# Pooled attention and a routed FFN on one core: the routing and the FFN moved a half pair, small operations swapped between GpSimd and VectorE, the last half reordered

## The chip, the core and the metric

The kernel runs on one core of one Trainium2 chip. The core has five engines that work side by side, each through its own list of instructions in order: TensorE (PE in the profile; its weight loads are a row of their own, PEld), VectorE (DVE), ScalarE (ACT), GpSimd (POOL) and SyncE (SP), which here only issues transfers. The metric is the time of one execution on the device, in microseconds (us); less is better.

## The reference, cut to what matters

All numbers are fp32. There are 8 batches with 8 heads, 1152 keys, and head width 64.

```python
# attention; queries are averaged in pairs: 1152 -> 576 per head
q_pool = q.reshape(B, H, S // 2, 2, D).mean(axis=3)
scores = scale * np.matmul(q_pool, k.transpose(0, 1, 3, 2))
attn = np.exp(scores - max) ; attn = attn / (sum + 1e-9)
attn_out = np.matmul(attn, v)                    # (8, 8, 576, 64)
x = attn_out -> (B, 576, 512)                    # heads side by side

# routed FFN: only 128 of a batch's 576 tokens pass through it
scores = np.einsum('bsd,d->bs', x, w_gate)
out = x.copy()
for b in range(B):
    top_idx = np.argpartition(-scores[b], 128)[:128]
    xe = x[b, top_idx]
    ye = np.maximum(xe @ w1, 0.0) @ w2           # 512 -> 1024 -> 512
    g = 1.0 / (1.0 + np.exp(-scores[b, top_idx]))
    out[b, top_idx] = x[b, top_idx] + g[:, None] * ye
```

## The kernel before

Heads are taken two at a time: 8 batches of 4 pairs make 32 pairs. A pair is worked in two halves of 288 queries, `s` = 0 and 1, so there are 64 halves, and half `h` belongs to pair `h // 2`. In half `h` TensorE computes the scores of half `h` (line 818, 9 blocks of 128 keys, ScalarE takes the exponents, line 825) and then the weighted values of half `h - 1` (line 836). So 8 halves after a batch's first one the next batch begins, and the routing and the FFN of a batch run between the halves of the batches behind it. `p` has two buffers, PSUM is used as four pairs of banks in turn (`banks()`).

What the other engines do in a half, in the order of the program:

```python
    def gated(self, half):              # of half h - 3
        nc.vector.tensor_reduce(pair["red"][:, ns], pair["prod"][:, ns, :], AX.X, ALU.add)   # L979
        if half["s"] == 1:
            nc.vector.tensor_tensor(out=pair["part"][:, pair["hp"], :],                      # L981
                in0=pair["red"][:, :], in1=pair["rec"][:, :], op=ALU.mult)
            if pair["hp"] == self.NPAIR - 1:      # a batch's last pair: its routing begins
                unit = self.routed(pair["b"], pair["part"])
                at = next(unit) == "mid"
                self.routing.append([pair["b"], unit, at])

    def folded(self, half):             # of half h: sums over the keys
        for u in range(G):              # G = 3
            nc.gpsimd.tensor_tensor(out=acc[:, u, :], in0=units[:, 0, u, :],                 # L857
                                    in1=units[:, 1, u, :], op=ALU.add)
        for a, of in enumerate((units[:, 2, :, :], acc[:, :, :])):
            nc.vector.tensor_reduce(fold[:, a, :], ..., apply_transpose=True)                # L862
        nc.vector.tensor_reduce(pair["sum"][:, :, ns], ...)                                  # L872

    # multiplied(h - 2): GpSimd, prod = avb * w_gate (L925)
    # prepare_pair, even halves: GpSimd qp (L732), VectorE transposes kT, qT (L735, L739)
    # weighted(h - 1): TensorE L836; ScalarE copies PSUM to `two` (L844); GpSimd av (L846)
    # drained(h - 1): VectorE transposes av to avb (L915)
    # added, even halves: VectorE `total` of the pair's sums (L893); spread: ScalarE L902

    def normalized(self, pair):         # odd halves
        ...
        rec = pair["rec"] = self.small.tile([P, self.QB], F32, name="rec")
        nc.vector.reciprocal(rec[:, :], tot)                                                 # L954
        x = self.work.tile([P, self.QB, BLK], F32, name="x")
        nc.gpsimd.tensor_tensor(out=x[:, :, :], in0=pair["avb"][:, :, :],                    # L956
            in1=rec[:, :].unsqueeze(2).broadcast_to([P, self.QB, BLK]), op=ALU.mult)
        pair["x"] = x
```

`routed` is a generator: each `yield` ends a piece, and its mark says where in a half the next piece is put. `"mid"` is behind the scores, `True` at the half's end; a false mark goes on at once.

```python
    def routed(self, b, part):
        mid = "mid" if b < self.B - 2 else True
        nc.vector.tensor_reduce(line[:, :], part..., AX.X, ALU.add)                          # L1007
        if b < self.B - 1:
            yield mid
            if b < self.B - 2:
                groups = self.side_by_side(line)          # ScalarE
                yield True
                total = self.added(groups)
            else:                                         # batch 6 alone
                nc.tensor.matmul(ps, lhsT=merge, rhs=line[:, :], ...)                        # L1021
                nc.scalar.copy(total[:, :], ps[0:BLK, :])
            ...                          # scores through DRAM and back as a line on all lanes
            yield True
            if b < self.B - 2:
                yield True
        else:                            # the last batch: diag (VectorE), L1054, columns (L679)
            ...
        for t, rows in tiles:            # ranks by comparison, 5 tiles: L1083, L1092, L1102
            ...
            if t == 1:
                yield True
            if t == 3:
                yield mid
                nc.scalar.activation(gate[:, :], gate[:, :], AF.Exp, scale=-1.0)
                if b < self.B - 2:
                    yield True
        ...                              # rank through DRAM to `lines`
                yield True
                for of, to in ((self.token_line, found), (lines[:, :, 1, :], own_gate)):
                    nc.vector.scalar_tensor_tensor(out=pick..., accum_out=to[0:w, :])        # L1166
                nc.gpsimd.tensor_scalar(out=index[0:w, :], in0=found[0:w, :],                # L1175
                    scalar1=float(b * Sp), scalar2=None, op0=ALU.add)
            nc.gpsimd.indirect_dma_start(out=xe[0:w, :], ...)         # gather of the rows, L1183
            yield True
            yield mid
            ...                          # 4 transposes of xe (L1197), ScalarE copies to xeT
            yield mid
            ...                          # layer 1: 8 pieces (L1208); marks False, last "hidden"
            ...                          # layer 2: 8 pieces (L1221); marks False
            ...                          # times the gate, plus xe, scatter
```

The loop over the halves, before:

```python
        for h in range(n_halves + 1):
            if h < n_halves:
                ...
                self.scores(half)
                ...                                 # side_by_side (even) or spread (odd)
                self.units(mid=True)
                if h > 2:
                    self.gated(halves[h - 3])
                self.folded(half)
                if h > 1:
                    self.multiplied(halves[h - 2])
                if s == 0 and loaded:
                    upcoming = loaded
                    self.prepare_pair(upcoming)
            else:
                self.stored(halves[h - 3]["pair"])
                self.gated(halves[h - 3])
                self.multiplied(halves[h - 2])
                self.units(mid=True)
                self.units(mid=False)
            if h > 0:
                done = halves[h - 1]
                self.weighted(done)
                self.drained(done)
            if h == n_halves:
                self.multiplied(done)
                self.gated(halves[h - 2])
            if 1 < h < n_halves and s == 0:
                done["pair"]["total"] = self.added(done["pair"]["groups"])
            if h == n_halves:
                self.normalized(done["pair"])
            elif h > 2 and s == 1:
                self.normalized(halves[h - 2]["pair"])
            if h < n_halves:
                self.units(mid=False)
```

So, counted from a batch's first half (r = 0), the routing begins at r = 10, the ranks are computed at the ends of r = 13, 14 and 15, the gather is issued at the end of r = 16, and transposes, layer 1 and layer 2 stand in the middle of r = 18, 19 and 20. Batch 5's layer 2 and the FFNs of batches 6 and 7 are kept for the end, where they fill TensorE's time while the last batch is routed.

Of the kernel before, what the change touches and what calls it, by code (L numbers as in the profile page):

```python
# [10 lines left out]
P = 128  # L11
BLK = 32
# [522 lines left out]
class _Plain:  # L535
# [396 lines left out]
    def normalized(self, pair):  # L932

        nc, hp = self.nc, pair["hp"]
        tot = self.sums[:, pair["b"] * self.NPAIR + hp, :]
        if self.last_pair(pair):
            ps = self.banks()[:, 0, :]
            nc.tensor.matmul(
                ps[:, 0 : 2 * self.QB],
                lhsT=self.merge.rearrange("p g j -> p (g j)"),  # L940
                rhs=pair["sum"].rearrange("p j n -> p (j n)"),
                start=True,
                stop=True,
            )
            for j in range(2):
                rows = slice(j * self.D, (j + 1) * self.D)
                nc.scalar.activation(
                    tot[rows, :],
                    ps[rows, j * self.QB : (j + 1) * self.QB],
                    AF.Identity,  # L950
                    bias=self.tiny[rows, 0:1],
                )
        rec = pair["rec"] = self.small.tile([P, self.QB], F32, name="rec")
        nc.vector.reciprocal(rec[:, :], tot)  # L954
        x = self.work.tile([P, self.QB, BLK], F32, name="x")
        nc.gpsimd.tensor_tensor(  # L956
            out=x[:, :, :],
            in0=pair["avb"][:, :, :],
            in1=rec[:, :].unsqueeze(2).broadcast_to([P, self.QB, BLK]),
            op=ALU.mult,  # L960
        )
        pair["x"] = x

    def stored(self, pair):

# [7 lines left out]
    def gated(self, half):  # L973

        nc, pair, hb = self.nc, half["pair"], self.HB
        if half["s"] == 0:
            pair["red"] = self.small.tile([P, self.QB], F32, name="red")
        ns = slice(half["s"] * hb, (half["s"] + 1) * hb)
        nc.vector.tensor_reduce(pair["red"][:, ns], pair["prod"][:, ns, :], AX.X, ALU.add)  # L979
        if half["s"] == 1:  # L980
            nc.vector.tensor_tensor(  # L981
                out=pair["part"][:, pair["hp"], :],
                in0=pair["red"][:, :],
                in1=pair["rec"][:, :],
                op=ALU.mult,
            )
# [10 lines left out]
    def routed(self, b, part):  # L997
# [139 lines left out]
        for s0, w in self.slots:  # L1137
# [3 lines left out]
            if b == self.B - 1:  # L1141

                nc.vector.tensor_tensor(
                    out=pick[:, :, 0:w],
                    in0=self.slot_f[:, s0 : s0 + w].unsqueeze(1).broadcast_to([P, NT, w]),
                    in1=rank[:, :].unsqueeze(2).broadcast_to([P, NT, w]),
                    op=ALU.is_equal,
                )
                yield True
                ps = self.banks()[:, 0, 0:2]  # L1150
                for t, rows in tiles:
                    nc.tensor.matmul(
                        ps[0:w, :],
                        lhsT=pick[0:rows, t, 0:w],
                        rhs=meta[0:rows, t, :],
                        start=(t == 0),
                        stop=(t == NT - 1),
                    )
                nc.scalar.copy(index[0:w, :], ps[0:w, 0:1])
                nc.scalar.copy(own_gate[0:w, :], ps[0:w, 1:2])  # L1160
            else:
                yield True

                found = self.small.tile([P, 1], F32, name="found_token")
                for of, to in ((self.token_line, found), (lines[:, :, 1, :], own_gate)):
                    nc.vector.scalar_tensor_tensor(  # L1166
                        out=pick.rearrange("p t i -> p (t i)").rearrange("p (i t) -> p i t", t=NT)[0:w],
                        in0=lines[0:w, :, 0, :],
                        scalar=self.token[0:w, s0 // P : s0 // P + 1],
                        in1=of[0:w, :, :],  # L1170
                        op0=ALU.is_equal,
                        op1=ALU.mult,
                        accum_out=to[0:w, :],
                    )
# [115 lines left out]
        )  # L1290
        return count_i

    def units(self, mid):


        for entry in self.routing[::-1]:
            b, unit, at = entry
            if b in self.waiting or at != mid:
# [6 lines left out]
            entry[2] = end in ("mid", "hidden") and b < self.B - 2  # L1305

    def run(self):
        nc = self.nc
# [10 lines left out]
            self.load_values(loaded)  # L1319
        self.load_gate()  # L1320
        weights = self.weight_loads()
        for h in range(n_halves + 1):
            if h < n_halves:
                n, s = divmod(h, 2)
                if s == 0:
                    pair = upcoming
                    if pair["hp"] == 0:
                        part = self.ffn.tile([P, self.NPAIR, self.QB], F32, name="part")
                    pair["part"] = part
                else:  # L1330
                    loaded = None
                    if n + 2 < len(pairs):
                        loaded = self.load_pair(*pairs[n + 2])
                        self.load_values(loaded)
                    if n > 1:
                        self.stored(halves[h - 4]["pair"])
                if h > 1:
                    next(weights, None)
                half = {"pair": pair, "s": s}
                halves.append(half)  # L1340
                self.scores(half)
                if h > 1:

                    of = halves[h - 2 - s]["pair"]
                    if s == 0:
                        of["groups"] = self.side_by_side(of["sum"].rearrange("p j n -> p (j n)"))
                    else:
                        self.spread(of)
                self.units(mid=True)
                if h > 2:  # L1350
                    self.gated(halves[h - 3])
                self.folded(half)
                if h > 1:
                    self.multiplied(halves[h - 2])
                if s == 0 and loaded:
                    upcoming = loaded
                    self.prepare_pair(upcoming)
            else:
                self.stored(halves[h - 3]["pair"])
                self.gated(halves[h - 3])  # L1360
                self.multiplied(halves[h - 2])
                self.units(mid=True)
                self.units(mid=False)
            if h > 0:
                done = halves[h - 1]
                self.weighted(done)
                self.drained(done)
            if h == n_halves:
                self.multiplied(done)
                self.gated(halves[h - 2])  # L1370
            if 1 < h < n_halves and s == 0:
                done["pair"]["total"] = self.added(done["pair"]["groups"])
            if h == n_halves:
                self.normalized(done["pair"])
            elif h > 2 and s == 1:
                self.normalized(halves[h - 2]["pair"])
            if h < n_halves:
                self.units(mid=False)
        for _ in weights:
            pass  # L1380

        self.stored(halves[-1]["pair"])


        self.gated(halves[-1])
        left = [unit for _, unit, _ in self.routing]
        new = left.pop()
        old = left.pop() if left else iter(())
        older = left.pop() if left else iter(())
        assert not left  # L1390
# [81 lines left out]
```

## Time and profile before

| | |
|---|---|
| time, median of 3 runs | 707.77 us (707.0 to 708.58) |
| span of the profiled run | 704.8 us |
| first score block starts | 8.8 us |
| last matmul ends | 698.4 us |
| TensorE clock granted | 0.998 |
| HBM traffic | 115 GB/s over the span |

A row of the profile's groups names the line, the engine, the operation, what it writes and reads with their shapes, how often it ran, its busy time in all and the mean of one in ns, and the idle time of the engine just before it with what ended it. These are the groups of the operations that the change touches:

```
L857 POOL TENSOR_TENSOR acc<-p 128x576 f32<-128x576 f32 x192 | 266.3, 1417 | 15.4 <-ACT p L825 15.1
L862 DVE TRANSPOSE_TENSOR_REDUCE fold<-p 128x54 f32<-128x1728 f32 x64 | 126.0, 1969 | 50.2 <-ACT p L825 50.2
L956 POOL TENSOR_TENSOR x<-avb,rec 128x576 f32<-128x576 f32 x32 | 37.1, 1159 | 40.3 <-DVE rec L954 27.9
L981 DVE TENSOR_TENSOR part<-red,rec 128x18 f32<-128x18 f32 x32 | 27.0, 845 | 1.1
L893 DVE TENSOR_REDUCE total<-groups 32x36 f32<-32x144 f32 (+1 forms) x37 | 12.0, 325 | 0.0
L954 DVE RECIPROCAL rec<-sums 128x18 f32<-128x18 f32 x32 | 7.2, 225 | 0.0
L1175 POOL TENSOR_SCALAR index<-found_token 128x1 int32<-128x1 f32 x7 | 6.4, 920 | 20.2 <-DVE pick L1166 20.2
```

The chain that ended last is followed back from the last instruction, at each step to what released it. Printed in order of time it gives start, length and what ran; `x72` are 72 matmuls. The timeline gives start, length, engine, line, operation and operands.

### The profile page before, as it was taken

The numbers are of one execution on the slowest core, as the hardware profiler recorded it, in microseconds if no ns is written. First come the engines' busy times: TensorE is split into PE (matmuls) and PEld (weight loads), VectorE is DVE, ScalarE is ACT, GpSimd is POOL, SyncE is SP. The second block draws the span as 40 slices with busy tenths as digits, with TensorE's granted clock in tenths as the row PEclk, the third lists the DMA queues.
The fourth block names the chain that finished last, engine by engine and source line by source line (L and its number), as shares of the span: only waits on it lengthen the run. The fifth ranks groups of instructions, "written<-read, shape, count | busy, mean of one in ns | idle before, by whom it ended". The sixth has DMA issues, their size and how long they took to land.

```text
span 704.8 us, 23397 instructions
## 1 busy us (share of the span) xinstructions
PE 694.4 (99%) x9948; PEld 516.8 (73%) x9948; DVE 496.5 (70%) x793; ACT 444.5 (63%) x963; POOL 485.1 (69%) x452
## 2 busy tenths in 40 slices
PE   8999999999999999999999999999999999999996
PEld 5668899996758866688656887578775787766573
DVE  3877777996559965498754988559774697689540
ACT  6677778777547775477746776467754777477210
POOL 5877777868658695586955779467874877686520
PEclk9999999999999999999999999999999999999999
DMA  8888887858486483756928468382775728432200
GB/s 175 172 178 180 171 166 137 146 116 161 85 149 111 85 162 75 145 97 111 172 40 159 81 129 160 66 148 61 161 130 85 135 56 169 83 72 62 45 31 35
DMA packets 389490, 82.86 MB, mean 118 GB/s; under 512 B 376640, under 2 KB 376640, under 8 KB 389376
## 3 DMA queue, kind: packets, MB, share of 16 engines
q1 hardware_dynamic: 387872, 76.49, 58.1%
q0 software_dynamic: 1280, 4.20, 1.8%
q8 instruction: 80, 1.31, 0.8%
q10 hardware_dynamic: 224, 0.59, 0.3%
q14 instruction: 34, 0.28, 0.1%
HBM read 69.65 MB, written 11.59 MB: 115 GB/s over the span
## 4 chain that ended last, share of the span: by engine, by line
PE 89%; POOL 5%; issue 2%; DMA 1%; ACT 1%; DVE 1%; SPq 0%; POOLq 0%; DVEq 0%; ACTq 0%
PE ps L836 36%; PE ps L818 36%; PE ps L1208 8%; PE ps L1221 7%; POOL acc L857 2%; ACT p L825 1%; DMA kb<-in_k_dram 1%; DMA xe<-out_dram,index 1%; PE ps L1197 1%; POOL prod L925 1%; POOL x L956 0%; POOL av L846 0%; DVE fold L862 0%; POOL index L1175 0%; SPq L759 0%
## 5 line engine op out<-in xcount | busy, mean ns | idle before, releaser
L825 ACT ACTIVATE p<-ps 128x576 f32<-128x576 f32 x576 | 320.2, 695 | 1.7 <-PE ps L818 1.3
L818 PE MATMUL ps<-qT,kT 64*64 64x288 f32 x4608 | 295.2, 404 | 0.2 <-ACT p L825 0.2
L836 PE MATMUL ps<-p,v_sb 64*64 64x288 f32 x4608 | 294.6, 403 | 0.0
L857 POOL TENSOR_TENSOR acc<-p 128x576 f32<-128x576 f32 x192 | 266.3, 1417 | 15.4 <-ACT p L825 15.1
L836 PEld LDWEIGHTS ps<-p,v_sb 64*64 64x64 f32 x4608 | 215.5, 133 | 65.3 <-ACT p L825 9.2
L818 PEld LDWEIGHTS ps<-qT,kT 64*64 64x64 f32 x4608 | 208.0, 132 | 73.0 <-ACT p L825 15.4
L862 DVE TRANSPOSE_TENSOR_REDUCE fold<-p 128x54 f32<-128x1728 f32 x64 | 126.0, 1969 | 50.2 <-ACT p L825 50.2
L862 DVE TRANSPOSE_TENSOR_REDUCE fold<-acc 128x54 f32<-128x1728 f32 x64 | 125.3, 1957 | 46.0 <-POOL acc L857 45.8
L844 ACT COPY two<-ps 128x576 f32<-128x576 f32 x64 | 40.9, 639 | 156.9 <-PE ps L836 143.8
L846 POOL TENSOR_TENSOR av<-two 128x288 f32<-128x288 f32 x64 | 51.2, 800 | 96.5 <-ACT two L844 94.9
L915 DVE STREAM_TRANSPOSE avb<-av 128x288 f32<-128x288 f32 x64 | 29.4, 460 | 66.5 <-POOL av L846 66.5
L956 POOL TENSOR_TENSOR x<-avb,rec 128x576 f32<-128x576 f32 x32 | 37.1, 1159 | 40.3 <-DVE rec L954 27.9
L1208 PEld LDWEIGHTS ps<-xeT,w 128*128 128x128 f32 x512 | 57.8, 192 | 2.7 <-ACT p L825 2.6
L1208 PE MATMUL ps<-xeT,w 128*128 128x128 f32 x512 | 59.3, 277 | 0.0
L1221 PE MATMUL ps<-w,hT 128*128 128x512 f32 x128 | 57.3, 598 | 0.0
L925 POOL TENSOR_TENSOR prod<-avb,w_gate 128x288 f32<-128x288 f32 x64 | 51.5, 805 | 0.6 <-DVE avb L915 0.6
L902 ACT ACTIVATE sums<-total,tiny 32x18 f32<-32x18 f32 x124 | 38.1, 308 | 15.9 <-DVE total L893 14.2
L732 POOL TENSOR_TENSOR qp<-qb 128x576 f32<-128x576 f32 x31 | 43.8, 1414 | 2.2 <-DMA qb<-in_q_dram 2.2
L1221 PEld LDWEIGHTS ps<-w,hT 128*128 128x128 f32 x128 | 23.6, 190 | 28.1 <-issue 25.8
L735 DVE STREAM_TRANSPOSE kT<-kb 128x1152 f32<-128x1152 f32 x31 | 42.5, 1370 | 0.0
L887 ACT COPY groups<-sum 32x36 f32<-32x36 f32 x124 | 27.1, 219 | 6.7 <-DVE sum L872 5.2
L981 DVE TENSOR_TENSOR part<-red,rec 128x18 f32<-128x18 f32 x32 | 27.0, 845 | 1.1
(95 smaller groups left out, 290.6 us busy)
## 6 DMA issues: line engine op xcount, KB each, us to landing
kb<-in_k_dram SPq DMA_DIRECT2D x124, 144.0 KB
qb<-in_q_dram SPq DMA_DIRECT2D x124, 144.0 KB
v_sb<-in_v_dram SPq DMA_DIRECT2D x124, 144.0 KB
out_dram<-x SPq DMA_DIRECT2D x128, 72.0 KB
lines<-row_rank SPq DMA_DIRECT2D x7, 640.0 KB
w<-in_moe_w_dram SPq DMA_DIRECT2D x8, 512.0 KB
sc_row<-row SPq DMA_DIRECT2D x7, 288.0 KB
acc<-in_q_dram ACTq DMA_DIRECT2D x2, 288.0 KB
```

What stands on the lines that cost most here:

```text
L732: nc.gpsimd.tensor_tensor(out=qp[:, :, :], in0=pair["q"][:, :, 0, :], in1=pair["q"][:, :, 1, :], op=ALU.add)
L735: nc.vector.transpose(kT.rearrange("p (c g i) -> p c g i", c=self.NC, i=BLK), pair["k"].rearrange("p (g c) d -> p c g d", c=self.NC),)
L818: nc.tensor.matmul(sc[keys, j, 0:n], lhsT=pair["kT"][rows, c * P + keys.start : c * P + keys.stop], rhs=pair["qT"][rows, qs], start=True, ...
L825: nc.scalar.activation(p[:, c // G, c % G, :, :], sc[:, :, 0:n], AF.Exp, scale=self.scale)
L836: nc.tensor.matmul(av[j * self.D : (j + 1) * self.D, e, 0:n], lhsT=half["pair"]["v"][keys, j, c, :], rhs=half["p"][keys, c // G, c % G, j, :],
L844: nc.scalar.copy(two[:, :, :], av[:, :, 0:n])
L846: nc.gpsimd.tensor_tensor(out=half["av"][:, :], in0=two[:, 0, :], in1=two[:, 1, :], op=ALU.add)
L857: nc.gpsimd.tensor_tensor(out=acc[:, u, :], in0=units[:, 0, u, :], in1=units[:, 1, u, :], op=ALU.add)
L862: nc.vector.tensor_reduce(fold[:, a, :], of.rearrange("p u (m d) -> p (u m) d", d=BLK), AX.X, ALU.add, apply_transpose=True,)
L925: self.nc.gpsimd.tensor_tensor(out=pair["prod"][:, ns, :], in0=pair["avb"][:, ns, :], in1=self.w_gate[:, hp : hp + 1, :].broadcast_to([P, ...
L1208: nc.tensor.matmul(pv[:, f, 0:w], lhsT=self.w1[:, c, (f0 + f) * P : (f0 + f + 1) * P], rhs=xeT[:, c, 0:w], start=(c == 0), stop=(c == self ...
L1221: nc.tensor.matmul(ps[0:w, 0 : self.Dm], lhsT=hT[:, f, 0:w], rhs=self.w2[:, f, :], start=(f == 0), stop=(f == self.NFC - 1),)
```

## The change

It regroups work without changing what is computed. `x` is computed by GpSimd half a pair later, at the end of the even half. The product of gate sums and reciprocals (`part`) moves from VectorE to GpSimd, except for the last two pairs, so that VectorE is relieved. The token index of the gather is computed by VectorE, so that GpSimd's queue doesn't stand waiting for it, and the gather is issued in the next half behind GpSimd's sums (a new place, `"sums"`, behind `folded`). Transposes and both layers of the FFN of batches 0 to 5 come one half later, to give the gather time. The first piece of the routing, `line`, also goes to the place `"sums"`. `total` is computed ahead of the transposes of the next pair's keys. The last half gets an order of its own, in which the value blocks of the last two halves follow each other and the products for the last batch's routing are ahead of `x`.

The diff, cut (`...`) where lines are only moved or indented:

```diff
-        rec = pair["rec"] = self.small.tile([P, self.QB], F32, name="rec")
-        nc.vector.reciprocal(rec[:, :], tot)
-        x = self.work.tile([P, self.QB, BLK], F32, name="x")
-        nc.gpsimd.tensor_tensor(
+        pair["rec"] = self.small.tile([P, self.QB], F32, name="rec")
+        nc.vector.reciprocal(pair["rec"][:, :], tot)
+
+    def divided(self, pair):
+        x = pair["x"] = self.work.tile([P, self.QB, BLK], F32, name="x")
+        self.nc.gpsimd.tensor_tensor(
...
         if half["s"] == 1:
-            nc.vector.tensor_tensor(
+            ending = pair["b"] == self.B - 1 and pair["hp"] >= self.NPAIR - 2
+            engine = nc.vector if ending else nc.gpsimd
+            engine.tensor_tensor(
                 out=pair["part"][:, pair["hp"], :],
...
             if pair["hp"] == self.NPAIR - 1:
-                unit = self.routed(pair["b"], pair["part"])
-                at = next(unit) == "mid"
-                self.routing.append([pair["b"], unit, at])
+                self.routing.append([pair["b"], self.routed(pair["b"], pair["part"]), "sums"])
...
-                nc.gpsimd.tensor_scalar(
+                nc.vector.tensor_scalar(
                     out=index[0:w, :],
...
+                yield "sums"
             xe = ffn.tile([P, self.Dm], F32, name="xe")
             nc.gpsimd.indirect_dma_start(
...
             yield True
-            yield mid
+            if b < self.B - 2:
+                yield True
+            if b != self.B - 2:
+                yield mid
...
-        for h in range(n_halves + 1):
+        for h in range(n_halves):
...
+            self.units("mid")
+            if h > 2:
                 self.gated(halves[h - 3])
+            self.folded(half)
+            self.units("sums")
+            if h > 1:
                 self.multiplied(halves[h - 2])
+            if h > 1 and s == 0:
+                last = halves[h - 1]["pair"]
+                last["total"] = self.added(last["groups"])
+            if s == 0 and loaded:
+                upcoming = loaded
+                self.prepare_pair(upcoming)
             if h > 0:
+                self.weighted(halves[h - 1])
+                self.drained(halves[h - 1])
+            if h > 2 and s == 1:
                 self.normalized(halves[h - 2]["pair"])
+            if h > 3 and s == 0:
+                self.divided(halves[h - 3]["pair"])
+            self.units("end")
...
-        pieces(older, self.NFC - 2)
+        self.gated(halves[-3])
+        self.weighted(halves[-1])
+        self.drained(halves[-1])
+        self.multiplied(halves[-2])
+        self.multiplied(halves[-1])
+        self.gated(halves[-2])
+        pieces(older, 1)
+        self.normalized(halves[-1]["pair"])
+        for half in (halves[-3], halves[-1]):
+            self.divided(half["pair"])
+            self.stored(half["pair"])
+        self.gated(halves[-1])
+        _, new, _ = self.routing.pop()
+        pieces(new, 1)
+        pieces(older, self.NFC - 3)
+        pieces(old, 1)
         pieces(new, 1)
         pieces(older, 2)
         pieces(new, 3)
```

More of the change, by code (lines that the diff above doesn't have):

```diff
@@ L952, in normalized @@
                 )
-        rec = pair["rec"] = self.small.tile([P, self.QB], F32, name="rec")
-        nc.vector.reciprocal(rec[:, :], tot)
-        x = self.work.tile([P, self.QB, BLK], F32, name="x")
-        nc.gpsimd.tensor_tensor(
+        pair["rec"] = self.small.tile([P, self.QB], F32, name="rec")
[3 more added lines that the diff above has]
+        self.nc.gpsimd.tensor_tensor(
             out=x[:, :, :],
             in0=pair["avb"][:, :, :],
-            in1=rec[:, :].unsqueeze(2).broadcast_to([P, self.QB, BLK]),
+            in1=pair["rec"][:, :].unsqueeze(2).broadcast_to([P, self.QB, BLK]),
             op=ALU.mult,
         )
-        pair["x"] = x
     def stored(self, pair):
@@ L1291, in outside, with units @@
         return count_i
-    def units(self, mid):
+    def units(self, at):
         for entry in self.routing[::-1]:
-            b, unit, at = entry
-            if b in self.waiting or at != mid:
+            b, unit, place = entry
+            if b in self.waiting or place != at:
                 continue
@@ L1304, in units, with place @@
                 self.waiting.add(b)
-            entry[2] = end in ("mid", "hidden") and b < self.B - 2
+            entry[2] = self.place(b, end)
+    def place(self, b, mark):
+        if mark in (True, None) or b >= self.B - 2:
+            return "end"
+        return "mid" if mark == "hidden" else mark
     def run(self):
@@ L1321, in run @@
         weights = self.weight_loads()
-        for h in range(n_halves + 1):
-            if h < n_halves:
-                n, s = divmod(h, 2)
+        for h in range(n_halves):
+            n, s = divmod(h, 2)
+            if s == 0:
+                pair = upcoming
+                if pair["hp"] == 0:
+                    part = self.ffn.tile([P, self.NPAIR, self.QB], F32, name="part")
+                pair["part"] = part
+            else:
+                loaded = None
+                if n + 2 < len(pairs):
+                    loaded = self.load_pair(*pairs[n + 2])
+                    self.load_values(loaded)
+                if n > 1:
+                    self.stored(halves[h - 4]["pair"])
+            if h > 1:
+                next(weights, None)
+            half = {"pair": pair, "s": s}
+            halves.append(half)
+            self.scores(half)
+            if h > 1:
+                of = halves[h - 2 - s]["pair"]
@@ L1325, in run @@
                 if s == 0:
[L1326 to L1329, printed above, removed]
-                else:
[L1331 to L1359, printed above, removed]
+                    of["groups"] = self.side_by_side(of["sum"].rearrange("p j n -> p (j n)"))
+                else:
+                    self.spread(of)
@@ L1360, in run @@
+            self.units("mid")
+            if h > 2:
                 self.gated(halves[h - 3])
+            self.folded(half)
+            self.units("sums")
+            if h > 1:
                 self.multiplied(halves[h - 2])
-                self.units(mid=True)
-                self.units(mid=False)
-            if h > 0:
[L1365 to L1375, printed above, removed]
+            if h > 1 and s == 0:
[4 more added lines that the diff above has]
+                self.prepare_pair(upcoming)
+            if h > 0:
+                self.weighted(halves[h - 1])
+                self.drained(halves[h - 1])
@@ L1376, in run @@
+            if h > 2 and s == 1:
                 self.normalized(halves[h - 2]["pair"])
-            if h < n_halves:
-                self.units(mid=False)
+            if h > 3 and s == 0:
+                self.divided(halves[h - 3]["pair"])
+            self.units("end")
         for _ in weights:
             pass
[L1382 to L1388, printed above, removed]
@@ L1389, in run @@
-        older = left.pop() if left else iter(())
-        assert not left
         def pieces(unit, n=None):
@@ L1395, in pieces @@
                     break
-        pieces(older, self.NFC - 2)
+        left = [unit for _, unit, _ in self.routing]
+        old = left.pop() if left else iter(())
+        older = left.pop() if left else iter(())
+        assert not left
+        self.gated(halves[-3])
[14 more added lines that the diff above has]
+        pieces(old, 1)
         pieces(new, 1)
```

## The prediction

> **What bounds the kernel now.** I read the page's first two parts, then the chain that ended last in order of time, then who waited for whom on TensorE, and last the timeline around the places where the chain leaves TensorE. First the page:
>
> ```profile
> PE 694.4 (99%) x9948; PEld 516.8 (73%) x9948; DVE 496.5 (70%) x793; ACT 444.5 (63%) x963; POOL 485.1 (69%) x452
> PE 89%; POOL 5%; issue 2%; DMA 1%; ACT 1%; DVE 1%; SPq 0%; POOLq 0%; DVEq 0%; ACTq 0%
> ```
>
> TensorE is the bound. As busy time alone can flatter it, I use lengths of blocks in the chain:
>
> ```profile
> 157.86 4.38 PE ps L836 x72
> 162.24 4.47 PE ps L818 x71
> 166.71 0.59 PE ps L1197 x4
> 167.30 4.53 PE ps L836 x72
> 171.82 4.37 PE ps L818 x72
> 176.19 7.34 PE ps L1208 x64
> 183.53 4.53 PE ps L836 x72
> 188.06 4.37 PE ps L818 x72
> 192.42 7.06 PE ps L1221 x16
> ```
>
> A score block and a value block take 4.37 each, so a half is 8.74 us; a batch's FFN adds 0.59 + 7.34 + 7.06 and three changes of shape of 0.16, some 15.5. So 64 x 8.74 + 8 x 15.5 = 683; with 8.8 ahead of the first scores and 6.5 behind the last matmul that is 698.6 of a span of 704.8. Only some 6 us are not needed work, so no reordering gains 2%; what matters is where TensorE stands still. Measured from start to start of blocks, the score block ahead of the transposes of the gathered rows (L1197) exceeds 4.37 by 0.31, 0.37, 0.44, 0.96, 0.43 and 0.85 in batches 0 to 5, 3.4 together. In batches 3 and 5 the rows come late; otherwise the bank does, since ScalarE's exponents have slipped:
>
> ```profile
> 418.75 0.27 issue
> 419.02 4.89 DMA xe<-out_dram,index
> 423.90 0.14 issue
> 424.04 0.63 PE ps L1197 x4
> ```
>
> The row gather lands only as TensorE arrives. Behind 640 us TensorE loses 0.8 at batch 6's transposes and 0.8 (0.46 + 0.35) ahead of L1054. The other engines have slack, but little: a half's VectorE work ends about a half late. The place that decides my number is half 58, where batch 6 is routed:
>
> ```profile
> 597.88 0.40 DVE L979 TENSOR_REDUCE red<-prod 128x9 f32<-128x288 f32 x1
> 598.32 0.92 DVE L981 TENSOR_TENSOR part<-red,rec 128x18 f32<-128x18 f32 x1
> 599.27 0.28 DVE L1007 TENSOR_REDUCE line<-part 128x18 f32<-128x72 f32 x1
> 599.47 1.97 DVE L862 TRANSPOSE_TENSOR_REDUCE fold<-p 128x54 f32<-128x1728 f32 x1
> 599.16 4.15 POOL L857 TENSOR_TENSOR acc<-p 128x576 f32<-128x576 f32 x3
> 600.79 0.40 PE L1021 MATMUL ps<-line,merge 128*128 128x18 f32 x2
> 601.12 4.59 PE L818 MATMUL ps<-qT,kT 64*64 64x288 f32 x72
> ```
>
> `line` is ready at 599.55 and its matmul L1021 follows at 600.79, between the values of half 57 and the scores of half 59. It has 1.2 us to spare, and only because `line` stands ahead of both folds.
>
> **What the skill says.** (1) The Trainium skill, "SBUF — State Buffer", section "Who interferes with whom": a VectorE operation with two SBUF inputs contends with GpSimd's reads. The trace agrees: `part`, 18 numbers a lane, takes 845 ns, the one-input reciprocal of the same size 225 ns. (2) "GPSIMD Engine Reference", section 3.1, has two-input work there bound by one read port at about 2.6 cycles an element plus dispatch; here 288 elements take 800 ns and 576 take 1417, 2.14 ns each and 0.18 fixed, so I estimate 0.25 us for `part` on GpSimd. (3) "TensorE: Matmul & The Clock Gate", section "The mechanism", has matmuls first in, first out. Here the wait at 424.04 holds the ready value block behind it, so a late L1021 holds the scores. (4) "Perfetto Trace Analysis", "Identifying the Most-Contended Engine", warns that matmul busy time misjudges the headroom; the 99% against 6 spare us agrees only because I counted blocks.
>
> **The change, part by part.** I count halves r from the first of a batch.
> - Index: one VectorE instruction of 0.15 (estimate from the 0.17 of a 128x5 reduction, L1124's group) in place of 0.92 on GpSimd, where it kept the queue idle for 2.97 (x7, 20.2 in all). The gather moves behind the next half's three sums. At half 57 those ran at 590.90 to 595.05, behind index and gather; now they start when GpSimd is free.
> - FFN a half later: transposes at r=19 instead of 18, layers at 20 and 21. The gather goes out about 3 us into half 18 in TensorE's time; with the 4.8 to 5.8 us seen from issue to landing and 11 us until the transposes, it is never late. The bank wait stays in part (normal halves meet their bank with no slack). Of the 2.5 us in batches 0 to 4 I credit 1.2, of the 0.85 in batch 5 0.75.
> - `x` a half later: GpSimd's 1.16 moves from odd to even halves and no longer waits for the reciprocal (27.9 us of idle). Off the path.
> - `part` on GpSimd: saves VectorE 0.85 x 30 = 25 us, but now stands ahead of the sums, so GpSimd can't begin `acc` until VectorE has done `red`. In half 54 of this batch `red` ends at 561.77, `acc` began at 559.84: a delay of 2.2. VectorE then waits for `acc` with its second fold.
> - `total` ahead of the transposes: 0.3, off TensorE's path.
> - `line` behind the folds (the place "sums"): harmless for batches 0 to 5, which use it a half later, not for batch 6.
>
> Worked for half 58, in times of the old trace. In half 54 `part` ends at 562.05, `acc` at 566.2 (4.15), so the second fold starts at 566.25 instead of 564.52: VectorE is 1.7 late. Through half 55 it stays so; in half 56 `red` ends at 580.6 and the sums start at 580.9 (578.54 before). Fold 585.1 to 587.0, then sum, total and transposes put qT at 589.65, against scores at 590.49: 0.8 to spare. The two `pick`s end at 591.6 (589.3), `red` at 592.2, first fold at 594.0. GpSimd sums half 57 from 589.1 to 593.25, before the second fold, so that one runs 594.0 to 595.95 (595.09 to 597.07 before): here the change gains 1.1. Sum, avb, rec, `red`: 597.2; `part` 597.5; `acc` of half 58 to 601.66; fold to 603.6, sum, `line` to about 604.2. TensorE, without the transposes and their wait, reaches L1021 at 590.49 + 8.74 = 599.2. It stands still for 5.1 us.
>
> The end: the values of half 63 follow those of 62 at once. Behind them stand one FFN step (0.88), the merge (0.24), five steps (4.41) and batch 6's transposes (0.6), 6.1 in all. The chain to L1054 is two 0.75, av 0.8, prod 0.75, prod 0.8, red 0.5, part 0.65, line 0.3, diag 0.76 = 5.3, as av is no longer behind x and an older prod. So that wait goes. What follows L1054 is as before.
>
> Sum: +5.1 at L1021; -1.2 and -0.75 at the transposes of batches 0 to 5; -0.8 at batch 6's; -0.8 ahead of L1054. Together +1.5: 707.77 + 1.5 = 709.3 us.
>
> **Rivals.** (a) The changed order works as meant: VectorE reaches half 58 without lag. Even then exponents of half 58 begin at about 591.8, the fourth is out at 593.7, three sums to 597.9, fold, sum and `line` to 600.5: a wait of 1.3. With all 5.0 us of the named waits (3.36 + 0.83 + 0.81) regained that is 707.77 + 1.3 - 5.0 = 704.1. For it speak the 20 us that GpSimd loses to the index; against it that VectorE is busy 16.8 of 17.5 us in the window from 127.0 to 144.5 (two halves), so a lag isn't made good at once. (b) GpSimd and VectorE, now chained twice per pair (red, part, acc, fold), become the bound where ranks are computed: the 0.8 left for qT in half 58 is used up and TensorE waits 0.5 to 1 us in each of six batches, and the two-input picks, which now run beside a busy GpSimd, add a microsecond to the wait at L1021: 713 to 716. Against it: FFN halves of 16 us let both catch up once a batch. (c) All is hidden and the sums cancel: 707 to 708.
>
> **Range and chances.** The stall at half 58 can be 2 to 7, the credit for the transposes 0.5 to 3.3, and (b) reaches upward: 705.0 to 713.0 for 8 in 10. Faster by 2% would need 693.6, below the 698.6 counted above; slower by 2% is 721.9, some 14 us of new waits, seven times the net sum and possible only if (b) comes in full. So 0.01, 0.95, 0.04.
>
> **What would show it.** L1021 starting 4 to 6 us after the value block ahead of it, with `line` behind the second fold and VectorE named in TensorE's waits; no DMA named ahead of L1197, and its score blocks within 0.3 of 4.37; `part` on GpSimd near 0.25 us, starting right behind `red`; no gap ahead of L1054. I'm wrong if L1021 starts less than 2 us late (then the time is near 705), or if score blocks of rank halves wait for qT (then over 712).

## The result, and the profile after

The changed kernel takes 711.57 us against 708.06 us of the kernel before, measured side by side: 1.0053 times as long, with a 95% interval of 1.0034 to 1.0071, so 2.4 to 5.0 us slower. The prediction was 709.3 us (705 to 713). The first two parts of the page and the shares of the chain that ended last, after:

```profile
PE 694.3 (98%) x9948; PEld 512.6 (72%) x9948; DVE 478.1 (67%) x770; ACT 446.3 (63%) x963; POOL 491.0 (69%) x475
PE 90%; DVE 3%; POOL 2%; DMA 2%; issue 1%; ACT 1%; SPq 0%; POOLq 0%; DVEq 0%; ACTq 0%
```

VectorE has lost 18 us of busy time and TensorE none; the span grew by 4.9 us all the same (704.8 to 709.7). Who waited for whom, on TensorE, after (total, times, longest, in us):

```profile
PE ps L1024 <- DVE line L1010: 5.5, 1, 5.5
PE ps L783 <- DMA kb<-in_k_dram: 1.4, 2, 1.1
PE ps L818 <- DVE qT L739: 0.4, 1, 0.4
```

L1024 is the merge matmul of batch 6, L1021 before. No gather of rows is named any more, nor the last batch's L1054. One long wait has taken the place of all of them. The timeline of half 58, after (start, length, engine, what):

```profile
596.52 0.39 DVE L981 TENSOR_REDUCE red<-prod 128x9 f32<-128x288 f32 x1
596.99 0.23 POOL L986 TENSOR_TENSOR part<-red,rec 128x18 f32<-128x18 f32 x1 [1.31 <-DVE red L981]
597.18 4.11 POOL L857 TENSOR_TENSOR acc<-p 128x576 f32<-128x576 f32 x3
601.32 1.98 DVE L862 TRANSPOSE_TENSOR_REDUCE fold<-acc 128x54 f32<-128x1728 f32 x1 [2.53 <-POOL acc L857]
603.59 0.26 DVE L1010 TENSOR_REDUCE line<-part 128x18 f32<-128x72 f32 x1
604.00 0.58 PE L1024 MATMUL ps<-line,merge 128*128 128x18 f32 x2 [5.54 <-DVE line L1010]
604.51 6.53 PE L818 MATMUL ps<-qT,kT 64*64 64x288 f32 x72
```

This is the chain that was worked out: red, part, sums, fold, `line`. TensorE had ended its values at 598.46. But the last row is news: the score block behind the wait takes 6.5 us instead of 4.4 (6.46 from its start to the start of what follows, which is how blocks are measured below). Busy times by stretch of the same execution tell why (stretch, its length, then busy us of PE, PEld, DVE, ACT and POOL, then the granted TensorE clock, the DMA share and GB/s):

```profile
593.90:598.40 4.50, 4.50 (x76) 3.63 (x72) 4.46 (x6) 2.34 (x7) 3.15 (x5) 1.00 0.85 169
604.00:608.40 4.40, 4.40 (x34) 2.47 (x38) 2.78 (x5) 2.12 (x4) 1.29 (x3) 0.50 0.06 8
608.40:611.00 2.60, 2.60 (x45) 1.36 (x37) 0.00 (x0) 2.31 (x5) 1.51 (x2) 0.99 0.83 148
```

TensorE's granted clock fell to half at 601.65, 3.2 us after its last value matmul, and stayed there for 6.8 us, the last 4.5 of them with TensorE at work again. The Trainium skill has this in "TensorE: Matmul & The Clock Gate", section "What's actually happening": the array runs at half rate after an idle window of about 3.4 us, and at full rate after a busy one as long. The trace agrees in kind at this place, with 3.2 us of standing still ahead of the drop and 4.5 us of work ahead of the full clock.

### The profile page after: what moved, and what is told of

It is laid out like the page before. It is cut to its first block, busy times and chain, and to the rows that moved or that the text cites. A ratio compares the mean times of both kernels' runs of the same rounds, so it can differ in the third digit from the quotient of the medians.

```text
span 709.7 us, 23364 instructions
## 1 busy us (share of the span) xinstructions
PE 694.3 (98%) x9948; PEld 512.6 (72%) x9948; DVE 478.1 (67%) x770; ACT 446.3 (63%) x963; POOL 491.0 (69%) x475
## 4 chain that ended last, share of the span: by engine, by line
PE 90%; DVE 3%; POOL 2%; DMA 2%; issue 1%; ACT 1%; SPq 0%; POOLq 0%; DVEq 0%; ACTq 0%
PE ps L836 37%; PE ps L818 37%; PE ps L1216 8%; PE ps L1229 7%; DMA kb<-in_k_dram 1%; POOL acc L857 1%; DVE fold L862 1%; PE ps L1205 1%; ACT p L825 1%; DVE tie L1105 1%; DMA v_sb<-in_v_dram 0%; DVE kT L735 0%; POOL av L846 0%; POOL prod L925 0%; DMA row_rank<-both 0%
## 5 line engine op out<-in xcount | busy, mean ns | idle before, releaser
L857 POOL TENSOR_TENSOR acc<-p 128x576 f32<-128x576 f32 x192 | 273.5, 1453 | 12.4 <-ACT p L825 12.3
L836 PEld LDWEIGHTS ps<-p,v_sb 64*64 64x64 f32 x4608 | 210.7, 133 | 70.1 <-ACT p L825 9.0
L986 POOL TENSOR_TENSOR part<-red,rec 128x18 f32<-128x18 f32 x30 | 6.7, 225 | 65.1 <-DVE red L981 61.9
L1224 ACT ACTIVATE hT<-ps 128x512 f32<-128x512 f32 x16 | 9.6, 597 | 39.1 <-PE ps L1216 39.1
```

Source lines behind the costliest of these rows:

```text
L836: nc.tensor.matmul(av[j * self.D : (j + 1) * self.D, e, 0:n], lhsT=half["pair"]["v"][keys, j, c, :], rhs=half["p"][keys, c // G, c % G, j, :],
```

## The experiments

Each time is a median; each ratio is to the kernel before, run on the same chip at the same time, with its 95% interval. Two kernels of different groups are compared by their ratios.

**1. Is it the line, and is it the clock?** Theory: the late `line` costs the wait, and the wait the slow block behind it. Rival 1: VectorE and GpSimd are chained too tightly everywhere, and the line only shows it. Rival 2: the slow block has a late input.

e1_line_first reduces batch 6's `line` ahead of the folds:

```diff
-                self.routing.append([pair["b"], self.routed(pair["b"], pair["part"]), "sums"])
+                unit, place = self.routed(pair["b"], pair["part"]), "sums"
+                if pair["b"] == self.B - 2:
+                    next(unit)
+                    place = "end"
+                self.routing.append([pair["b"], unit, place])
```

> The changed kernel, but batch 6's line is reduced ahead of the folds of half 58, as before; all else as changed. Theory (the late line costs 5.5 us of standing still, and the standing still slows the score block behind it by 2.1 us): both go, 7.6 us less, so 711.6 - 7.6 = 704.0 us, L1024 within 1.5 us of its value block, the score block of half 59 at 4.4 to 4.5 us. Rival 1 (VectorE and GpSimd are chained more tightly everywhere, and the late line only shows the lag): part of the lag remains, TensorE waits elsewhere, 707 to 709 us. Rival 2 (the slow score block has another cause, such as a late qT): the block stays at 6.5 us, 706 us.

Measured: 702.97 us, 0.9951 (0.9936 to 0.9967). Against the changed kernel's 1.0053 that is 1.02% or 7.2 us less, against the 7.6 expected. The timeline of half 58:

```profile
596.96 0.28 DVE L1014 TENSOR_REDUCE line<-part 128x18 f32<-128x72 f32 x1 [0.34 <-POOL part L986]
598.08 0.40 PE L1028 MATMUL ps<-line,merge 128*128 128x18 f32 x2
```

`line` now waits 0.34 us for GpSimd's `part` and is there 0.8 us before TensorE wants it. The next score block takes 4.53 us. In this execution TensorE waits for nothing behind its start. Rival 1 falls as an account of the loss. Together with e12_index_gpsimd below, which has the same ratio, it is the fastest version: 0.5% faster than the kernel before.

e2_filled_wait leaves the line late and fills the time with matmuls whose result isn't used:

```diff
+                for _ in range(6):
+                    nc.tensor.matmul(both_banks[:, 1, :], lhsT=self.ones[:, :],
+                                     rhs=self.w1[:, 0, 0:512], start=True, stop=True)
                 nc.tensor.matmul(ps, lhsT=self.merge..., rhs=line[:, :], ...)
```

> The changed kernel with six matmuls of 128x512 more (0.88 us each, 5.3 us, result not used) ahead of L1024, in the time in which TensorE stands still. Theory (standing still drops TensorE's clock): the score block of half 59 takes 4.4 to 4.6 us instead of 6.5, while L1024 still starts when line is there; 2 us less, 709.5 us. Rival 2 (qT, a bank or ScalarE is late behind L1024): the block stays at 6.5 us and the time at 711.6 us.

Measured: 708.79 us, 1.0033 (1.0017 to 1.0049). The same stretches:

```profile
597.80:603.40 5.60, 5.50 (x16) 2.20 (x12) 3.02 (x5) 0.64 (x1) 5.60 (x6) 1.00 0.00 0
603.40:608.20 4.80, 4.75 (x74) 2.95 (x74) 2.93 (x5) 3.72 (x8) 2.58 (x4) 1.00 0.28 60
```

The line is as late as before, and the score block behind it runs at the full clock and takes 4.52 us, not 6.46. So 1.9 us of the loss are the clock, and rival 2 falls. The times alone show it less sharply (the two intervals overlap); the block and the clock carry it.

e3_before_line_late is the converse: the kernel before with nothing but batch 6's line moved behind the folds.

```diff
+                if pair["b"] == self.B - 2:
+                    self.late = unit          # its first piece runs behind self.folded(half)
```

> The kernel before, with only batch 6's line put behind the folds of half 58. Its last fold of half 58 ended at 605.32, with sum and line that is 606.0, and L1021 stood at 600.79: 5.2 us of standing still. Theory: 5.2 + 2.1 for the slow block, less about 0.8 that the waits near the end give back: 708.1 + 6.5 = 714.6 us. Rival 1 (the stall comes from part on GpSimd and the lag it makes): here part is on VectorE, so the stall stays under 3 us and the time under 711.5 us.

Measured: 713.99 us, 1.0103 (1.0087 to 1.0118), 7.3 us slower. On TensorE:

```profile
PE ps L1024 <- DVE line L1010: 4.8, 1, 4.8
PE ps L1200 <- DMA xe<-out_dram,index: 1.6, 2, 1.0
```

The block behind takes 6.95 us. One instruction moved behind three others (two folds and their sum) costs as much as the late `line` of the changed kernel did (5.5 and 1.9 us), without any of the other changes. Rival 1 falls here too, since `part` is on VectorE and the wait is 4.8 us all the same.

**2. What are the other parts worth?** The prediction had put several of them down as off TensorE's path.

e4_part_vector is the changed kernel with `part` on VectorE again:

```diff
-            engine.tensor_tensor(
+            nc.vector.tensor_tensor(
```

> The changed kernel with all gate sums times reciprocals on VectorE again. Theory: in half 58 GpSimd needn't wait for red (1.3 us idle), but VectorE has 0.85 us more work, so line comes 0.5 to 2 us earlier; the stall of 5.5 falls to 3.5 to 5, the slow block may stay: 709.5 to 711.5 us. Rival 1 (the chain through part is what costs): the stall falls below 2 us and no score block waits for qT: 704 to 706 us.

Measured: 730.80 us, 1.0349 (1.0308 to 1.0390), 2.9% slower than the changed kernel with its 1.0053. Neither account had this. The timeline of half 26 in it (rows for PE, DVE and POOL):

```profile
256.02 9.83 DVE L984 TENSOR_TENSOR part<-red,rec 128x18 f32<-128x18 f32 x1
257.70 0.79 POOL L925 TENSOR_TENSOR prod<-avb,w_gate 128x288 f32<-128x288 f32 x1
258.45 1.39 POOL L732 TENSOR_TENSOR qp<-qb 128x576 f32<-128x576 f32 x1
259.82 0.79 POOL L846 TENSOR_TENSOR av<-two 128x288 f32<-128x288 f32 x1
260.57 1.15 POOL L959 TENSOR_TENSOR x<-avb,rec 128x576 f32<-128x576 f32 x1
261.69 4.12 POOL L857 TENSOR_TENSOR acc<-p 128x576 f32<-128x576 f32 x3
272.52 0.76 PE L818 MATMUL ps<-qT,kT 64*64 64x288 f32 x4 [5.06 <-DVE qT L739]
```

A product of 18 numbers a lane, 0.18 us at the shortest in this run, takes 9.8 us. GpSimd goes from `acc` to prod, qp, av, x and the next three sums without a gap, and `part` ends just as the last of them does. Everything behind it on VectorE is late, and TensorE waits 5.1 us for qT. This happens twice (10.2 us in all), and each time the clock is halved for 6.8 us.

e8_x_later_alone tests that reading: the kernel before, with only `x` moved to the end of the even half, which closes GpSimd's gap, and `part` on VectorE.

```diff
             elif h > 2 and s == 1:
                 self.normalized(halves[h - 2]["pair"])      # now the reciprocal alone
+            elif h > 3:
+                self.divided(halves[h - 3]["pair"])         # x
```

> The kernel before with only x a half later, so that GpSimd has qp, av, x and the next sums in one row in even halves, and part still on VectorE. Theory (a VectorE instruction with two inputs waits as long as GpSimd goes from one instruction to the next without a gap, as the 9.9 us of part in e4_part_vector show): the longest part takes 4 us or more, and TensorE waits for qT at least once: 709 to 725 us. Rival (part was starved in e4_part_vector because the gather and the index had moved): no part over 3 us, time within 1 us of before.

Measured: 721.16 us, 1.0189 (1.0155 to 1.0224). The group of `part` in its profile (of the kernel before it read 27.0 us, mean 845 ns):

```profile
L983 DVE TENSOR_TENSOR part<-red,rec 128x18 f32<-128x18 f32 x32 | 70.2, 2192 | 1.1
```

Six of the 32 take over 2 us, one in each of six batches, the longest 10.5. So the starving comes with x in the even half, and not with the gather or the index, which are where they were. That a row without a gap is enough for it isn't shown, though. In the kernel before, too, another two-input operation of GpSimd follows without a gap in 25 of the 32 cases, and `part` still gets in at the end of the one that it meets. In e8_x_later_alone the six long ones began 0.42 to 0.44 us into a sum of GpSimd's; those that began 0.59 to 0.74 us into one waited for that one alone. What decides is open. The theory also had wrong where it surfaces: no wait for qT, but ScalarE standing up to 9.7 us for `total`, and TensorE waiting 6.1 us in all for ScalarE ahead of score blocks and 3.6 us for batch 6's `line`.

e5_ffn_later is the kernel before with only the FFN of batches 0 to 5 a half later:

```diff
             yield True
+            if b < self.B - 2:
+                yield True
             yield mid
```

> The kernel before with only the transposes and layers of batches 0 to 5 one half later (gather and index where they were). Theory (the waits ahead of the transposes are worth what the changed kernel showed at them): the score blocks ahead of the transposes fall from 3.4 us over 4.37 to about 1.0 in all six batches, no DMA is named ahead of L1197 before 640 us; 2.0 to 2.4 us less: 704.6 us. Rival (the wait only moves, as ScalarE is the cause): under 1 us less, 706 us.

Measured: 733.12 us, 1.0360 (1.0331 to 1.0390): 25 us slower where 2.0 to 2.4 less were expected. Its waits on TensorE, and on ScalarE:

```profile
PE ps L818 <- ACT xeT L1202: 9.0, 5, 2.0
PE ps L818 <- ACT two L844: 3.2, 5, 0.8
ACT sums L902 <- DVE total L893: 45.3, 16, 4.6
```

In the odd half ScalarE has to spread `total`, which VectorE computes behind both transposes. Before, the copy of the transposed rows stood in the even half; now it stands in ScalarE's queue behind that wait, and with it the copies and exponents that free TensorE's banks. In half 35 the sums start at 359.97 after 4.6 us of standing, `two` follows at 362.50 and the first exponents at 363.04, 3.6 us after their score block began. TensorE stands 2.0 us, from 360.64 on, and over the 5.0 us from 363.0 on its clock is 0.66. Four batches have such a standstill of 2.0 us, and in two of them the clock was halved behind it. The 25 us are spread over many blocks: the score blocks of the five batches concerned take up to 8.6 us instead of 4.4.

e6_new_ending is the kernel before with only the new order of the last half (the diff of the changed kernel for it).

> The kernel before with only the last half's new order (values of 62 and 63 together, products ahead of x, batch 6's transposes behind five FFN steps). Theory: the 0.8 us ahead of batch 6's transposes and the 0.8 us ahead of the last batch's first matmul (L1054) go: 1.6 us less, 705.2 us. Rival (the chain from the last values to L1054 is still longer than the work that stands in between): 0.8 us less, 706.0 us.

Measured: 706.52 us, 0.9981 (0.9968 to 0.9993), 1.3 us less (0.5 to 2.3). The times alone don't tell the theory's 1.6 from the rival's 0.8. The profile has no wait of TensorE but two at the start, so both waits at the end went.

e7_both_alone joins e5_ffn_later and e6_new_ending.

> The kernel before with the FFN a half later and the new ending, and nothing else: x, part, index, total and line as before. Theory (these two are all that the change brings, and the swaps between GpSimd and VectorE are off TensorE's path): 702.8 to 703.4 us, as e1_line_first. Rival (index and part off their old engines are worth something of their own): 704.5 us or more.

Measured: 731.42 us, 1.0352 (1.0313 to 1.0391), within the noise the loss of e5_ffn_later. That the rest of the change is idle work is refuted.

e9_later_total_first adds `total` ahead of the transposes to e5_ffn_later, and e10_and_new_ending the ending to that:

```diff
+                if h > 1 and s == 0:
+                    last = halves[h - 1]["pair"]
+                    last["total"] = self.added(last["groups"])
                 if s == 0 and loaded:
                     upcoming = loaded
                     self.prepare_pair(upcoming)
```

> e5_ffn_later with total ahead of the transposes of keys and queries as well (the kernel before with these two changes). In e5_ffn_later ScalarE stood 3 to 4.6 us in front of the sums, as VectorE computed total behind both transposes, and the copies of PSUM and the exponents came behind them in ScalarE's queue. Theory: total 2.3 us earlier takes most of that away: no wait of TensorE on xeT or two over 0.5 us, 704 to 707 us, against 733 of e5_ffn_later. Rival (the lag of VectorE and GpSimd as such is the cause, whichever instruction shows it): 715 us or more.

> e9_later_total_first with the new ending: the kernel before with three of the change's parts (FFN later, total first, ending), and x, part, index and line as before. Theory: e9_later_total_first less 1.6 us, so 702.5 to 705.5 us, at or a little above e1_line_first (703.0). If the swaps between GpSimd and VectorE are needed to make the FFN's place work, 2 us or more above e1_line_first.

Measured: 719.64 us, 1.0163 (1.0129 to 1.0197), and 718.09 us, 1.0132 (1.0107 to 1.0157). `total` early regains about half of e5_ffn_later's loss, not nearly all, so both times are where the rival had them. On TensorE in e9_later_total_first:

```profile
PE ps L818 <- ACT two L844: 4.2, 4, 1.1
PE ps L1021 <- DVE line L1007: 3.2, 1, 3.2
PE ps L818 <- DVE qT L739: 2.5, 4, 0.6
```

There even `line` ahead of the folds is 3.2 us late, for VectorE as such is behind. e1_line_first differs from e10_and_new_ending in x, part, index, the gather's place and the line of the other batches, and is 1.8% or 13 us faster. Those parts together carry the FFN's new place.

e11_total_last is e1_line_first with `total` behind the transposes, and e12_index_gpsimd e1_line_first with the index on GpSimd (each undoes that part of the change's diff).

> e1_line_first with total behind the transposes again, where it was before. Theory: in the changed kernel, too, ScalarE needs total early; the sums in odd halves wait 1 to 2.5 us more, and where the FFN's copy follows them TensorE waits: 706 to 720 us. Rival (with part and index moved VectorE is early enough): within 1 us of e1_line_first, 703 to 704 us.

> e1_line_first with the index on GpSimd again, 0.92 us there and a wait of 1 to 3 us for the picks, ahead of the sums of the next half. Theory: GpSimd's standing costs the sums of half 57 and its like about 3 us, but only part of it reaches TensorE: 703 to 706 us. Rival (moving the index is worth nothing): 703.0 us, as e1_line_first.

Measured: 708.50 us, 1.0003 (0.9990 to 1.0017), and 704.28 us, 0.9951 (0.9929 to 0.9973). `total` ahead is worth 0.5%, some 3.7 us: without it the score blocks ahead of the first layer exceed 4.37 us by 0.9 in five batches. The index alone is worth nothing that is measured; L1028 waits 0.7 us for `line` in its profile and the rest is slack.

## Why the prediction was right, and where it was not

**The bound and its size.** TensorE was the bound and only some 6 us were to be had, so no new order gains 2%: the best one gained 0.5%. A loss of 2% needed some 14 us of new waits (nine times the net sum of 1.5, not seven), and the changed kernel has 3.5. The caution that single parts could cost more was missing: e5_ffn_later alone lost 3.6%.

**The line of batch 6.** The step "it stands still for 5.1 us" was right in place, mechanism and size: 5.54 measured. e1_line_first and e3_before_line_late show it from both sides. Counted from the start of half 58's scores, VectorE's `red` ended at 7.4 us (worked out: 6.7), the sums at 11.8 (11.2), and the merge matmul began at 14.5 (13.7). `part` took 0.23 (estimated as 0.25; its own two shapes give 0.22). The 0.8 us by which the chain came later go with the two picks: beside GpSimd's sums they took 3.0 us instead of 1.7, as rival (b) had feared. TensorE itself was 0.3 us slower through half 58, so the wait grew by 0.4 only. The sums of half 57, beside the picks, took 5.3 us instead of 4.15, but they ended at 592.80, 1.0 us before VectorE came to the fold that reads them, and cost nothing here.

**What was left out of the sum** is the clock. The step that failed is the sum itself, which let TensorE go on at full speed after 5.1 us of standing, and so came to +1.5 us where +3.5 was measured. The block behind it took 6.46 us against 4.53 in e1_line_first: 1.9 us, shown by e2_filled_wait. I had taken from that page only the order of matmuls.

**Transposes of batches 0 to 5.** "I credit 1.2" was low by half a microsecond: the blocks in batches 0 to 4 exceed 4.37 by 0.84 together instead of 2.51, so 1.7 came back. But 0.65 were lost again in batch 3, where a comparison on VectorE took 3.25 us beside two sums and a product of GpSimd and qT came 0.4 us late: rival (b) in one batch of six. That the two nearly offset each other, so that the sum of 1.95 for all six batches came out, was luck. TensorE reached half 58 at 589.49 instead of 590.49, 1.0 us earlier. The profiles of e1_line_first and e2_filled_wait have no such wait, so it doesn't come in every execution of this order.

**The end.** Both waits went as worked out, 0.83 at batch 6's transposes and 0.81 ahead of the last batch's first matmul; e6_new_ending alone measured 1.3. The margin was thinner than the 5.3 against 6.1 us worked out: diag, with two inputs, took 1.35 us instead of 0.76 beside `x` and ended at 668.99, L1057 began at 669.14.

**The account** of the profiled 4.9 us: +5.5 and +1.9 at half 58, -1.7 and +0.65 in batches 0 to 4, -0.85 in batch 5, -0.8 and -0.8 at the end, and a rest of 0.9 in small pieces from half 58 on, not followed up. The prediction's +1.5 differs by 0.4 of the wait, 1.9 of the clock, 0.1 of the transposes and these pieces. The medians of the timed runs differ by 3.5; the profiled execution of the kernel before was one of its faster ones.

**"Off the path"** was the weakest reading: said of `x` and of `total`, it held only because other parts of the change support these two. `total` ahead is worth 3.7 us inside the change; x a half later costs 13 us (1.9%) unless `part` leaves VectorE; and the FFN's new place costs 25 us without its companions. I had costed `part` as 25 us of VectorE time saved against a later start of the sums. What moving it buys inside the change is that it no longer starves on VectorE beside a row of GpSimd's instructions (e4_part_vector: 2.9%). How the 13 us between e10_and_new_ending and e1_line_first divide between x, part and the gather's place wasn't told apart.

## What to carry to other kernels

Before moving a small operation to a later place, ask who is the next to need it, in each case of the loop: here the one batch whose matmul stands in TensorE's queue right behind lost 7.2 us, twice what the rest of the change gained. An engine's idle share says little about what a move costs; what counts is which queue stands behind it, for an operation "off the path" is part of the path as soon as an in-order queue puts a copy that TensorE needs behind it. Parts of such a change should be judged together and undone one at a time, and a version that wins here is the change with one line put back.

## What the runs showed that I had not expected

- A standstill of TensorE can be paid twice: 5.5 us idle were followed by 4.5 us of work at half clock, which cost another 1.9 us. Shorter ones did it too, but not each time. Of ten standstills of 2.0 to 2.1 us in e5_ffn_later and e7_both_alone, five were followed by a halved clock. The 2.13 us ahead of batch 6's merge matmul were in e5_ffn_later (the clock fell 1.6 us after work had resumed, and its mean over the next 6.2 us of work was 0.72), and the same 2.13 us in e7_both_alone were not. Where it came behind standstills of 2.0 to 3.2 us, the half clock lasted 3.4 us, behind those of 3.6 to 5.5 us it lasted 6.8, and no standstill under 2.0 us had one (the longest of these is 1.87 us, in e8_x_later_alone). So the drop didn't need the idle window of about 3.4 us named above; here the measurement decides. What decides between two standstills of the same length wasn't tested.
- A VectorE operation with two SBUF inputs can wait not for one GpSimd instruction but for a whole row of them: `part` took up to 9.9 us in e4_part_vector and 10.5 in e8_x_later_alone, while in the kernel before none took over 0.92, and each ended with the one GpSimd instruction that it met, though in 25 of 32 cases another followed without a gap. "SBUF — State Buffer", section "Who interferes with whom", names the contention; that it can outlast one instruction is what these runs add; when it does is open. It goes the other way as well: with two picks running beside it, two of GpSimd's sums took 2.0 us each instead of 1.4.
